# The order table of a fused retention and two-MLP kernel, replaced by another order of the same operations

## The chip, the cores and the metric

The kernel runs on one core of one Trainium2 chip. The metric is the device time of one execution, in microseconds (us): the median of several runs, shown with the lowest and the highest of them. One more execution was taken with the hardware profiler, and every row below is from that one.

## The reference

```python
# retention: B=2, H=8, S=768, D=64
gamma = 1.0 - 2.0 ** (-5.0 - np.arange(H))
for t in range(S):
    state = gamma * state + einsum('bhd,bhe->bhde', k[:, :, t], v[:, :, t])
    y[:, :, t] = D ** -0.5 * einsum('bhd,bhde->bhe', q[:, :, t], state)
x = y.transpose(0, 2, 1, 3).reshape(B * S, H * D)          # 1536 x 512

# MLP 1: w_in 512 x 2048, w_out 2048 x 512
h = x @ w_in
P = a[0] + a[1]*h + a[2]*h**2 + a[3]*h**3
Q = 1.0 + abs(b[0])*abs(h) + abs(b[1])*h**2
x = (P / (Q + 1e-6)) @ w_out

# MLP 2: the same sizes
h = x @ w_in2
out = (h / (1.0 + exp(-h))) @ w_out2
```

Everything is in fp32.

## The kernel before

**Retention.** The 768 positions of the two batches make 12 chunks of 128 (chunk c is position block c // 2 of batch c % 2). A chunk loads kT, qT, vn and kn (128x512 each) and goes through these operations. The *scores* are 16 matmuls of kT with qT (L435) into two PSUM banks. Two *masks* on VectorE (L317, tile `am`, in some chunks `u2` and `w`) multiply the scores with the causal decay in `msk`. The *decay of kn* is eight small scalings (L421), on ScalarE for the first chunks, which read their factors from `cst`. The *growth* is 16 matmuls of kn with vn (L468) and is what the state `bd` gains. The *outputs* are matmuls of vn with the masked scores (L480), and from the third chunk on with the state as well (L490). They land in bank `h1`, the growth in bank `h0`. ScalarE copies the outputs to `xh` (L309) and VectorE subtracts that copy to get `xl` (L317). These two are the high and the low half of x in the matmul format fp32r.

**The two MLPs.** Tokens form three groups of 512 (four chunks each), and d_ff is cut into 16 blocks of 128. That gives 96 *steps*, 48 for each layer. A step has a *first product* (L526): 12 matmuls of 128x512 into bank `h0` or `h1`, by turns of the step's number. They are three products, high by high, high by low and low by high, over four slices of d_model. Then comes a chain on ScalarE and VectorE (the rational function in layer 1, tanh and a multiplication in layer 2), which ends in `gh` and `gl`, and last the *accumulations* (L576): three matmuls into each of the four banks `acc0` to `acc3`, which are added up over the 16 blocks and then emptied. Bank h0 is free for the step after next only when the chain has read it for the last time.

**Weights.** A weight comes by DMA into one of three buffers `raw` (L343). ScalarE makes two pieces of it (`wt` and `raw`, L309), of which the second adds a constant, VectorE joins them (L324), ScalarE writes the high half (`ih`, `oh`, L386) and GpSimd or VectorE the low half (`il`, `ol`, L391). A weight that is needed again after its place is given away goes to DRAM as `spill` and comes back from there. All loads and stores are issued from SyncE (SP), in one queue. Two loads are tiny: `par` (the parameters of the rational function, broadcast to 128 partitions) and `cst`.

**What sets the order.** The program first lists all operations, each with the buffers that it reads and writes. Then `Flow.order()` decodes the table `ORDER`, a compressed list of 16-bit operation numbers, and the operations are emitted in that order:

```python
places = np.frombuffer(zlib.decompress(base64.b85decode("".join(ORDER))), np.uint16)
done = [self.ops[n] for n in places]
assert all(o.place < f.place for o in done for f in o.feeds)
...
with tc.manual_schedule():
    for o in flow.order():
        o.emit()
```

So an engine takes its instructions, and SP its transfers, strictly in the order of the table, and an instruction that has to wait holds up everything behind it on its engine. No other rule decides the order; the times and ranks that stand beside an operation in the code are not read when the table is used.

Of the kernel before, what the change touches and what calls it, by code (L numbers as in the profile page):

```python
# [27 lines left out]


ORDER = (  # L30
    'c-jru0|Foi3;@75d$w)cwr$(CZQHhO+qP}nZhtWo8bUxghyd|G03j>@gooG=2TsFoU?2zyksvZeflv@1B0?C53eh13oPo2D020ADhz5ILFT{lN',
    '5DWG}Lf8*!AQhy9xR4VvLM})RhanxLhYXMyl0ZJl1Zm+SB!`2L6pq3XNCqh&3uK4<Pymj>aVP;LArF*>+)x2Z!DYw{Wg#z|giBBm%D^G02&W(i',
    '6oz7O6|O*5C=cZz8&rZqP#lUtWdICNp#~g)n$R3-K`UqhwSf?^8ic@*_!f%7HMkB{fYG2TR0qLOSQqL+eYg!b!6AV6@D2<cKpk+r1+5`8HiCw5',
    '1H$78D2y$kJ#>d25FIbTNazWl;4^%Huy_aV!aaBZjiD(tgNPUbi{MAN4^1EvK7>c`7-C`!EQ)O)GIoG)*cLiMJLm*Y;3>qyV)zV-V{GgU@$m~p',
    '#jo%jzCl+giCv%@e1{*<2l_%UP#g}Wu`-6i5;zk^z%+=0<6s!X!7^AD6JSEDidFChl)~N+4f{h9OoU0XA5_C~SRKpbE69k6F&QSuOqdz7;7fP|',
    'uVDZTgxXjEr^9ks4dZbc)W8`q9DhOz%!Vm3J66P+m=%XW4$O&hu@2V7R5%m{K`zXVzn~J1f?7BW;^9B|4UKUEHo?@`6er>c9EpQrH2i_TP!IFq',
    'Sg4O<pcziW7B~tg<7k|Y^RY3F!3MY##zPwHiW6Z1q{p<_9J^t6%!|FSCHBCEI0ahaRP2eZaV$=PsW2IOV;`J}eK8+4!f7}TGhlv9hi$Me&V~Y5',
    '2;1RuY(fig1}?;v*dAA4KkSbKa1IQ_dC&m|;ZEF*yKoWC!o@fjR^b|4i>q-R?!mpd9{1sF+>aY@0d&MJI2ecFd?<*Wa3gNQ%Xk2n;z2xwO=&aE',
    '#l_H!4&xDA0t=xzJ;g<^0y^UmT!I~G6SSfpGzB-p9K4EG@CIJPo45+D<1>7LTW}f9!!>XVZ{te1gU|6OcB0nQhF)SXx{LSl6~4x{)R~UqR@{bb',
    'VI6$Oq4);h;t%XeKk+`E!sB=Xx8n|MM_s5Zy~FqT0Z(Il`h&mlH@2XU_yAkdCk#m!@GL&W-t-s$VIK-b>mdwnfW@?mPU0EdNI>ThDKssmix`%c',  # L40
    'P&gtAPZ200ZH7nq7@y#0WD@F2+n@s}^`qFdj3QBFib7jpD=eq9^aZ!WH@t*9=sd2b%@l{?QdHVRYbXJwqg@b>64F}QLhC3R#i#U?h!WF!+5s!*',
    'D;hb4pcoWTblOUpC<A4tB$SkPLNa<xuP7sBp{&%6c2RQ5M%gI`ZJ?FZol?+i+DZB84LzlTRDgC<MT$wWXb-)mcT|K5(KdQQIjJ%gre{=?icvLs',
    'PSt5I6{lRZk3LdjPD!aL4W**Il#g;#9x6d4sTB36&-95ZQBr<SNw^ACrP5S`zR*`n#x<!H)uuW$fCkbx8bU9qE)Al=G?a!>8TvpksUCf&a#WVe',
    '(?qI3^{Ejxqy{vcM$jahLL+GuO{L^KnWoWnO2uh-2F;|@oPtNw7}`!Lc|Xmf*))d^&_OyvhbS!{rHk}~a_~4BOXFz*0neqJoQp5fW%@-w=`bCm',
    'd31%Y(RKPw$LT5|-=LfHhfdH*O2?<@77;5m8%N{?w2)3ydXB_V_%;bUpP>w#k>|-mxkCX*=DQS?V{lB)#F_aXh2Ur$opW<Y4#lxJ3+Lhaw201A',
    'elE!8=mMRk0$h<F(F1x&p}7zj=J}GB|59wu%0;*+hv9r&j4N?vj>B<zkrd~6{EzNaIBw11IV@M<YFvV=b4f16ZMiDf;F?^T+i)4K#kIK|ci_I<',
    'j}veNPRQ-KKR4FXGFyJ|8R^8?c#hQJ1=5ih%K#q4gL$sh<)+%1vvWPZBIhKKi?T!#ae1!5<2gPL<RLtiCvX?;%H8;^Oyns%m51>p?#?~91ux|D',
    'vWUxZS#HYpxe;&X#oUZr@^D_l%XkDg;K@9V8}mqB&P#bZui%y3oEvg0Zo)Ho6mR7%e3X0gF`mh*couKt*}R>1@eV%0t9cHu;a)tNdvhNi%VT&P',
    '@8r3BosaWLKEu2DEU)ELe3~!F9^T9Acpu;7{d|MZ@p-<*clfH@=6k$U?(zX%z%O||&*SxcpI`At4lSGbFmK=^e1WgY8-Bpc<RZW3w|q%H@Fjl8',
    '@Ay4G;?zp|Pgwr)ZwVtGIjlV9PaIAn$P@m|mnEXal|y`$4{~^kB=ID^B#<whNd8D<0sYDeCA}n(zmiy@NK*O6$t0?z)60B~3(6IK%Fp>3zu@nj',  # L50
    'K{84v$s*Atxn!0?l1-vZb}1rRC5BWMk{pskib`QACOM_JG?fyPMpH_9ts*7mC#RBJQcX%pX%Q(Sf7m6qRF|sKOj<}S$t^9Vjf9X4`j68}Old25',
    '1U0RO6qVW%OKM1SsUvaZ7uS^3QdU|?8UZOMtlg!xnADX}GE&+}PwA|x^`wWimp;-<^2sRaEBU3jjFB$7T>41|87sfJzo1Nz0n%E#YDE!UA?akG',
    'WYLT|QS!<vsV@a&kgS&S(m+f*$|R{EqotEnl65j!8p}!<CrxCqbkjz%UdBrsZ76G`t?rZ|l2zAACY>T1WU92&>#|#>$u8L_`(%%Flbf<%y2=gN',
    'B%Nii+>w`ZKyJxFxhuED^`0D(CfZ$x$}2f6bG3`ymmc~?hD%R<Ae$x7UiwzH$Pt;ZGv%SYmJ!lSL+Cr1E+6EP%#x4tUWQ3?jj2Z^l(x{8+FOrF',
    'Xl<n-HJpag9TH1F$qWgv?RBfn)6X(hAImoBpkcM6o{}fhS5HVMjicKowjP%+5?7x|1f8zgG`oJ4h?+p-=`>BK-z2_1m7JPcPf8Arq%Wk8=F!Mn',
    'Qgdlu&8-VGpGMLA+E0H-X-%YqwUqYPayn3#>HsaHgS5Ps)$g)UpG#t0tj9H~F47q~MwjUlU9L%VrY6+_T0wuxTAiiIbhiGIA-Y1N=^Txr(RHjA',
    ')QXy1SL!-Vp+ohYuGdvMPE+a$t)yG^q!!ZET3HM08oi+Vbc3GPD!NgtY7yP6S9Oz~(p0)di|a5grWduSp4JjtO|R)4y`*Qfu3p#S`c-RbJw2<{',
    '^|IF223lKh=r$dtSG10f*X?>&N9sMDppW&N-qihiU;pTLJ)jNsht|-^+DLckB(15p^nt$7+xk$&{^~#dsgLxRhO*H*LU-yE{jCReqCQczr@C9s',
    '!1icpJEXfbjG-OXx9XPI$o6Vjd!~n#?VTRe_j*JF3uh56gr&0Qn$$8{NK0bjEt$o#NEX2&TN+DlsqKSCu^g7k(%K8nY*Fo%rm%GOQe#^dt7soJ',
    'y`{7`_F8k=XU%H4?2~4&xK_iyXf}&sxvi3Ax5}2^@>mtCW%Vtd)wB{;)e2Z%t8LA!n&q>CR><mDbZcPMt)ca|m{!*kT1hKx(X55lvr?AGnp=D;',  # L60
    'ZH+8}wX^|N%o^K3Yh`V%i4C_h*4oBfQyXO6tev&7_BO%>+eqtRLu`~yx1m<VI@&}lZli62mA7HG(Z<>sn`9NNyN$D=HrdMB4C`S#ZN5#lDb~}b',
    '*(U2{n{B3Tu`ag2W?5I;Wm|29?Y4z>(ze?++haRyua&dew%_(yKU--B?SL(^Io8Qm*<9;vi>;QQwt05ZPFY=FZD(wa9k#P}$f|oEJ7<^dh%LAC',
    'cG>#c1-oTO?YJGYu71LL+iiPockGHa@T>O4-q>6FYqh<G*YTR(+k5y1TVl&>tu3`{cGuR~JzH;I?Ye!lcXrd>+kN|I?%)sXp@sKu-qX8#FAo)j',
    '4Q|*A`)(iXhrP6?_R0ePY$5!a{j}#6!ynlndu-^R?8*Nq`)I!{f`{~o{>vJAC})r4jXa^p^vGV%gCLgI_kJGQ6S;X}7f<DxT|Jz~_AuVZ<9Jx_',
    '>#048M+nk*5|8HnJ*nsM0iMN^23b9-7xm~K-_v?rPv`MGuP5+)p3Jj(InVCJytpU#6rR#Ecz#ds1w50N_l#b_b9)KT<t4q1=kUf}#G80dZ|ViT',
    'q7U>+-qzdsC@<xOy{s4VYTnGtcyq7pgS@H__7*<dOM7c??^V2mxAGz0(MS7G@9blIj<@u=zQo7+IPc<1Jw(vSmwD)5n1>AJd6;0hrwHczcuyUy',
    '^$9-FxA{6>?;|{AFw&C+se(zKJXr2ieT7f<1wO^6`F3CE(|w1}@cq8QXZl8;<tO}rAM}g9$`|=!U+Fu2jfV?%`6dq^ob=V6E;!{|{g7|=h{0js',
    ';*o+&zQ-^7X}{&^gEO8Xc<i_Rj_>t1e$4mzc|Y#E{it8@Bc3L>>gPOdaM#cJ6Tjy-{Hee73;xc(`ZIs-*ZrIS^Y8x9ulY^C@9+JUfA9zY7dUc&',
    'L7d=`fA$~#+JE{>j}m<GsKFo482t4Y{>dr$=p6j^Xu&U!8$=H@h!<oEB#0km4srzv0uOQrF@ijS1qp*JLF^!F5GzO$#0+u<d4t43z93PMEhrJ>',
    '2ucR|gHl2Epg>SGC>Rt9iUq}k!a<SXKT#GXzW',  # L70
)


# [663 lines left out]
```

## Time and profile before

| | before |
|---|---|
| median of 3 runs | 600.87 us (598.21, 601.35, 600.87) |
| the profiled execution | 599.9 us |
| its span in the trace | 598.1 us |
| mean granted clock of TensorE | 0.991 of full speed |
| busy: PE, DVE, ACT, POOL | 579.3, 426.7, 396.9, 134.8 us |

PE is TensorE (its matmuls), PEld its weight loads, DVE is VectorE, ACT ScalarE, POOL GpSimd, and SP the queue of transfers. The span runs from the first to the last instruction of the trace; the profiled execution's time is 1.8 us longer, for what lies around it. A busy time counts from the start to the end of instructions, and matmuls are pipelined, so a matmul shows a longer duration than the distance to the next one. A granted clock of 1.0 is 2.4 GHz, one of 0.5 is 1.2 GHz.

### The profile page before, as it was taken

Reading aid. Unit: us, or ns where it says so; the run is one execution under the profiler, and the core shown is the slowest. Engines: PE = TensorE matmul, PEld = TensorE weight load, DVE = VectorE, ACT = ScalarE, POOL = GpSimd, SP = SyncE. Lnnn points to the kernel's source line nnn. Section 1 sums busy time; section 2 is a strip of 40 time slices with the busy share of each in tenths; the row PEclk is TensorE's granted clock in tenths of the full one; section 3 lists DMA queues with packets and bytes.
Section 4 is the critical chain, followed back from the end, with each engine's and each line's share of the span. In section 5 each row is a group of like instructions: output and inputs, shape, how many; then the busy total and the mean of one; then the engine's idle time right before and its main releaser. Section 6 shows DMA issues by size and latency. Waiting matters only on the chain.

```text
span 598.1 us, 8106 instructions
## 1 busy us (share of the span) xinstructions
PE 579.3 (97%) x2950; PEld 475.6 (80%) x2950; DVE 426.7 (71%) x646; ACT 396.9 (66%) x690; POOL 134.8 (23%) x104
## 2 busy tenths in 40 slices
...
GB/s 291 326 330 302 337 140 169 169 134 78 105 72 81 96 1 105 18 19 107 53 106 158 176 135 187 195 222 176 71 89 36 1 1 0 106 18 1 0 2 71
DMA packets 33368, 70.02 MB, mean 117 GB/s; under 512 B 3632, under 2 KB 3632, under 8 KB 33328
## 3 DMA queue, kind: packets, MB, share of 16 engines
...
## 4 chain that ended last, share of the span: by engine, by line
PE 57%; DVE 17%; DMA 13%; ACT 9%; issue 2%; SPq 2%; ACTq 0%; DVEq 0%
PE acc L576 28%; PE h L526 27%; DMA raw<-in_moe_w_in_dram 6%; DVE wt L324 4%; DVE s L324 3%; DMA raw<-in_moe_w_out_dram 3%; DMA spill<-wt 2%; SPq L343 2%; DVE s L317 2%; DVE gl L317 1%; ACT wt L309 1%; ACT raw L309 1%; DVE u L324 1%; DVE t L324 1%; DVE r L324 1%
## 5 line engine op out<-in xcount | busy, mean ns | idle before, releaser
L526 PE MATMUL h<-xh,ih 128*128 128x512 f32 x384 | 150.7, 392 | 2.2 <-DVE s L324 1.9
L526 PE MATMUL h<-xl,ih 128*128 128x512 f32 x384 | 149.5, 389 | 0.0
L526 PE MATMUL h<-xh,il 128*128 128x512 f32 x384 | 149.5, 389 | 0.0
L317 DVE TENSOR_TENSOR gl<-w,gh 128x512 fp32r<-128x512 f32 x48 | 34.2, 712 | 82.5 <-ACT gh L309 82.4
L526 PEld LDWEIGHTS h<-xh,ih 128*128 128x128 f32 x384 | 72.1, 188 | 20.7 <-DVE s L324 3.6
L526 PEld LDWEIGHTS h<-xh,il 128*128 128x128 f32 x384 | 72.1, 188 | 15.1
L526 PEld LDWEIGHTS h<-xl,ih 128*128 128x128 f32 x384 | 72.1, 188 | 14.5
L309 ACT ACTIVATE gh<-w 128x512 fp32r<-128x512 f32 x48 | 30.2, 629 | 80.3 <-PE acc L576 77.0
L576 PE MATMUL acc<-oh,gh 128*128 128x512 f32 x192 | 74.8, 390 | 1.4 <-DVE xl L317 1.4
L576 PE MATMUL acc<-gh,oh 128*128 128x512 f32 x192 | 75.9, 395 | 0.0
L576 PE MATMUL acc<-gh,ol 128*128 128x512 f32 x192 | 74.8, 390 | 0.0
L576 PE MATMUL acc<-gl,oh 128*128 128x512 f32 x192 | 74.8, 390 | 0.0
L576 PE MATMUL acc<-ol,gh 128*128 128x512 f32 x192 | 74.7, 389 | 0.0
L576 PE MATMUL acc<-oh,gl 128*128 128x512 f32 x192 | 74.7, 389 | 0.0
L391 POOL TENSOR_TENSOR ol<-wt,oh 128x512 fp32r<-128x512 f32 x28 | 40.0, 1431 | 119.3 <-ACT oh L386 114.9
L324 DVE SCALAR_TENSOR_TENSOR w<-w,h 128x512 f32<-128x512 f32 x48 | 32.8, 685 | 37.6 <-ACT w L309 37.0
L324 DVE SCALAR_TENSOR_TENSOR wt<-wt,raw 128x512 int32<-128x512 int32 x64 | 50.4, 796 | 10.4 <-ACT wt L309 5.7
L309 ACT ACTIVATE raw<-raw,par 128x512 int32<-128x512 uint32 x64 | 48.4, 761 | 10.0 <-DMA raw<-in_moe_w_in_dram 5.2
L309 ACT ACTIVATE w<-h 128x512 f32<-128x512 f32 x48 | 28.3, 593 | 35.9 <-PE h L526 25.0
L317 POOL TENSOR_TENSOR gl<-s,gh 128x512 fp32r<-128x512 f32 x26 | 35.2, 1356 | 69.9 <-ACT gh L309 47.0
L309 ACT ACTIVATE wt<-raw 128x512 f32<-128x512 f32 x64 | 42.2, 666 | 12.3 <-DMA raw<-in_moe_w_in_dram 5.3
L324 DVE SCALAR_TENSOR_TENSOR s<-s,par,h 128x512 f32<-128x512 f32 x65 | 48.2, 743 | 0.9
...
## 6 DMA issues: line engine op xcount, KB each, us to landing
...
```

The costliest lines, as they stand in the source:

```text
L309: lambda: nc.scalar.activation(out=out_, in_=in_, func=func, **kw),
L317: op(eng, dur, rank, lambda: e.tensor_tensor(out=out_, in0=in0, in1=in1, op=alu), reads, writes, port)
L324: lambda: nc.vector.scalar_tensor_tensor(out=out_, in0=in0, scalar=scalar, in1=in1, op0=op0, op1=op1),
L343: op("swdge" if swdge else "sync", us, rank, lambda: e.dma_start(out=out_, in_=in_), reads, writes)
L391: e.tensor_tensor(out=sl.t[nm + "l"][:, us], in0=wt.t, in1=sl.t[nm + "h"][:, us].bitcast(F32), op=ALU.subtract)
L526: nc.tensor.matmul(h.t, sl.t[w][:, ws], x[g].t[:, c, :], start=(n == 0), stop=(n == 3 * KD - 1))
L576: nc.tensor.matmul(a.t, a1, a2, start=(first and n == 0), stop=(last and n == 2))
```

## The change

Only the strings of the table `ORDER` differ. The operations, their buffers and what each computes are the same, and so is the number of instructions on every engine. What differs is the place of an operation in its engine's queue: of PE's 515 operations 430 stand at another number than before, of ACT's 659 565, of DVE's 646 530, of GpSimd's 100 58, and of SP's 203 transfers 166.

```diff
@@ -28,46 +28,46 @@
 ORDER = (
-    'c-jru0|Foi3;@75d$w)cwr$(CZQHhO+qP}nZhtWo8bUxghyd|G03j>@gooG=2TsFoU?2zyksvZeflv@1B0?C53eh13oPo2D020ADhz5ILFT{lN',
...
+    'c-jru0}dbw5CFh-&)T+a+qP}nwr$(CZQHhO`|cB!R0s$Kp&=Zch6sQV2f{*Z0Eh?SVK=0Lj6lE;5+XrlhyrKeEJTDb5FZjiA~**LAsR%5J+K#I',
...
 )
```

The largest shift is at the start. On SP, the queue of transfers, these are the first eleven before (qT, kT, kn and vn are the chunks' inputs, `raw_2` of `moe_w_out` and `raw_0` of `moe_w_in` the first weights, the number in a name is that of the buffer):

```order
L343 DMA qT_0_168<-in_qt_dram 128x512
L343 DMA kn_0_162<-in_k_dram 128x512
L343 DMA kn_1_163<-in_k_dram 128x512
L343 DMA par_65<-in_moe_a_dram 128x4
L343 DMA cst_63<-in_consts_dram 128x48
L343 DMA kT_0_171<-in_kt_dram 128x512
L343 DMA msk_64<-in_consts_dram 128x1024
L343 DMA vn_0_165<-in_v_dram 128x512
L343 DMA kT_1_172<-in_kt_dram 128x512
L343 DMA qT_1_169<-in_qt_dram 128x512
L343 DMA raw_2_126<-in_moe_w_out_dram 128x1024
```

and these after the change:

```order
L343 DMA qT_0_168<-in_qt_dram 128x512
L343 DMA raw_2_126<-in_moe_w_out_dram 128x1024
L343 DMA kn_0_162<-in_k_dram 128x512
L343 DMA cst_63<-in_consts_dram 128x48
L343 DMA qT_1_169<-in_qt_dram 128x512
L343 DMA kT_0_171<-in_kt_dram 128x512
L343 DMA kT_1_172<-in_kt_dram 128x512
L343 DMA msk_64<-in_consts_dram 128x1024
L343 DMA kn_1_163<-in_k_dram 128x512
L343 DMA vn_0_165<-in_v_dram 128x512
L343 DMA raw_0_124<-in_moe_w_in_dram 128x2x512
```

The first half of a weight pair now stands second, both kT follow each other at the places 6 and 7, kn_1 has moved from the third to the ninth place, vn_0 from the eighth to the tenth, and `par` from the fourth to the 28th.

On ACT, these are the first instructions of the program before (L421 decays kn, L309 on `wt` and `raw` are the pieces of a weight, `xh0` is the copy of the outputs of chunk 1, `bd0` the state):

```order
L421 ACT_TABLE_LOAD
L421 ACTIVATE kn_1_163<-kn_1_163,cst_63 128x64 x8
L421 ACTIVATE kn_0_162<-kn_0_162,cst_63 128x64 x8
L309 ACT_TABLE_LOAD
L309 ACTIVATE u2_0_132<-u2_0_132,par_65 128x1
L309 ACTIVATE bd0_160<-h0_155 64x4x64 x2
L309 ACTIVATE wt_2_129<-raw_2_126 128x512
L309 ACTIVATE raw_2_126<-raw_2_126,par_65 128x512
L309 ACTIVATE wt_0_127<-raw_0_124 128x512
L309 ACTIVATE raw_0_124<-raw_0_124,par_65 128x512
L309 ACTIVATE xh0_66<-h1_156 128x4x128
```

and after the change:

```order
L309 ACT_TABLE_LOAD
L309 ACTIVATE wt_2_129<-raw_2_126 128x512
L309 ACTIVATE raw_2_126<-raw_2_126,par_65 128x512
L421 ACTIVATE kn_0_162<-kn_0_162,cst_63 128x64 x8
L309 ACT_TABLE_LOAD
L309 ACTIVATE u2_0_132<-u2_0_132,par_65 128x1
L421 ACTIVATE kn_1_163<-kn_1_163,cst_63 128x64 x8
L309 ACTIVATE wt_0_127<-raw_0_124 128x512
L309 ACTIVATE raw_0_124<-raw_0_124,par_65 128x512
L309 ACTIVATE xh0_66<-h1_156 128x4x128
L309 ACTIVATE bd0_160<-h0_155 64x4x64 x2
```

ACT's first instructions now read `raw_2` and no longer `kn_1` and `cst`; the two decays of kn lie between the pieces of the first two weights, and the copy to `bd0` comes behind xh0.

On DVE, this is the place in step 36's chain (layer 1, third group) where bank h0 (`h0_155`) is read for the last time, before (`raw` here holds the sums of the first group, `il` is a low half of a weight):

```order
L317 TENSOR_TENSOR raw_2_126<-acc1_152,raw_2_126 128x512
L317 TENSOR_TENSOR gl_1_147<-s1_1_137,gh_1_144 128x512
L391 TENSOR_TENSOR il3_85<-wt_1_128,ih3_84 128x512
L391 TENSOR_TENSOR il2_81<-wt_4_131,ih2_80 128x512
L317 TENSOR_TENSOR s1_0_136<-s1_0_136,h0_155 128x512
L324 SCALAR_TENSOR_TENSOR t_0_141<-u2_0_132,r_1_140 128x512
L324 SCALAR_TENSOR_TENSOR s1_0_136<-s1_0_136,par_65,h0_155 128x512
```

and after the change:

```order
L317 TENSOR_TENSOR raw_2_126<-acc1_152,raw_2_126 128x512
L391 TENSOR_TENSOR il2_81<-wt_0_127,ih2_80 128x512
L391 TENSOR_TENSOR il3_85<-wt_1_128,ih3_84 128x512
L324 SCALAR_TENSOR_TENSOR r_0_139<-t_1_142,r_0_139 128x512
L324 SCALAR_TENSOR_TENSOR u2_0_132<-w_0_134,par_65,h0_155 128x512
L317 TENSOR_TENSOR s1_0_136<-s1_0_136,h0_155 128x512
L324 SCALAR_TENSOR_TENSOR s1_1_137<-s1_1_137,par_65,r_1_140 128x512
L324 SCALAR_TENSOR_TENSOR s1_0_136<-s1_0_136,par_65,h0_155 128x512
L324 SCALAR_TENSOR_TENSOR s1_2_138<-s1_2_138,par_65,r_0_139 128x512
L317 TENSOR_TENSOR gl_1_147<-s1_1_137,gh_1_144 128x512
```

The last row of the first piece is the last read of h0 for step 36, after which PE may write the bank again. It stands at row 369 of DVE before and at row 362 after; `gl_1`, and the low half from `wt_4`, which stood ahead of it, now stand behind it.

On PE, the shifts that matter are these. Chunk 5's scores stood ahead of step 0's first product and now stand behind it. In chunks 0 and 1 the outputs now stand ahead of the growth. Between the first products of steps 2 and 3 there are three accumulations where there was one. At step 36 to 40, other matmuls have moved ahead of the first products of steps 38 and 40 (9 more of them, 2.0 us, and 18 more, 4.1 us). In the second layer most first products stand some accumulations later than before. The end of the program is practically the same.

## Rows read from the trace of the kernel before

**Rows 1.** The page: busy time of each engine, share of the span, instructions.
```profile
PE 579.3 (97%) x2950; PEld 475.6 (80%) x2950; DVE 426.7 (71%) x646; ACT 396.9 (66%) x690; POOL 134.8 (23%) x104
```

**Rows 2.** Busy time in three long stretches; the last columns are clock, DMA, GB/s.
```profile
core 0: us, PE busy (x) PEld busy (x) DVE busy (x) ACT busy (x) POOL busy (x), PEclk, DMA share, GB/s
0.00:60.00 60.00, 47.82 (x467) 40.97 (x468) 41.67 (x72) 43.83 (x93) 25.59 (x25) 0.91 0.90 313
60.00:280.00 220.00, 218.78 (x1111) 177.50 (x1111) 211.68 (x328) 193.96 (x329) 72.88 (x55) 1.00 0.33 110
280.00:598.00 318.00, 312.69 (x1375) 257.16 (x1373) 173.35 (x250) 159.07 (x269) 36.33 (x24) 1.00 0.27 85
```

**Rows 3.** Whom PE waited for: us in total, times, longest.
```profile
PE h L526 <- DVE s L324: 1.9, 3, 0.9
...
```

**Rows 4.** The same columns as rows 2, in the first 15 us.
```profile
0.00:4.00 4.00, 2.52 (x12) 2.52 (x13) 0.54 (x2) 0.00 (x0) 1.19 (x6) 1.00 0.57 162
4.00:6.00 2.00, 2.00 (x12) 1.96 (x11) 0.00 (x0) 0.00 (x0) 0.00 (x0) 1.00 0.67 113
6.00:7.00 1.00, 0.15 (x2) 0.00 (x0) 0.00 (x0) 0.26 (x1) 0.00 (x0) 1.00 0.84 314
7.00:15.00 8.00, 5.82 (x54) 5.32 (x56) 1.75 (x4) 7.92 (x23) 0.00 (x0) 0.63 1.04 398
```

**Rows 5.** The same columns, in the two stretches with the low clock.
```profile
9.10:15.80 6.70, 5.46 (x46) 5.12 (x48) 2.19 (x5) 6.63 (x19) 0.00 (x0) 0.50 1.01 376
46.60:49.90 3.30, 3.18 (x34) 2.88 (x35) 2.30 (x5) 2.32 (x5) 1.77 (x2) 0.50 1.03 387
```

**Rows 6.** PE's timeline, first 60 us: start, duration, instruction [idle before, releaser].
```profile
7.79 1.16 PE L435 MATMUL a<-qT,kT 64*128 64x128 f32 x16 [1.65 <-DMA kT<-in_kt_dram]
...
10.34 2.14 PE L468 MATMUL h<-vn,kn 128*64 128x64 f32 x16 [1.38 <-ACT kn L421]
...
19.42 0.32 PE L480 MATMUL h<-u,vn 128*64 128x128 f32 x1 [1.53 <-DVE u L317]
...
31.86 0.47 PE L526 MATMUL h<-xh,ih 128*128 128x512 f32 x1
...
39.61 1.09 PE L480 MATMUL a<-am,vn 128*64 128x128 f32 x16
...
43.96 1.16 PE L435 MATMUL a<-qT,kT 64*128 64x128 f32 x16 [1.56 <-DVE bd L317]
46.72 1.12 PE L468 MATMUL a<-vn,kn 128*64 128x64 f32 x16 [1.59 <-DVE am L317]
47.59 1.95 PE L480 MATMUL a<-am,vn 128*64 128x128 f32 x16
```

**Rows 7.** PE's timeline, later: matmuls in a row, and three waits.
```profile
261.71 0.39 PE L576 MATMUL acc<-gl,oh 128*128 128x512 f32 x1
...
262.39 0.39 PE L576 MATMUL acc<-gl,oh 128*128 128x512 f32 x1
263.42 0.50 PE L526 MATMUL h<-xh,ih 128*128 128x512 f32 x1 [0.65 <-DVE s L324]
...
270.87 0.50 PE L526 MATMUL h<-xh,ih 128*128 128x512 f32 x1 [0.35 <-DVE s L324]
...
343.64 0.51 PE L576 MATMUL acc<-oh,gh 128*128 128x512 f32 x1 [1.35 <-DVE xl L317]
```

**Rows 8.** ACT's timeline in the first 18 us, same columns.
```profile
6.74 1.28 ACT L421 ACT_TABLE_LOAD   x1 [6.74 <-DMA cst<-in_consts_dram]
8.03 3.92 ACT L421 ACTIVATE kn<-kn,cst 128x64 f32<-128x64 f32 x16
...
14.24 0.67 ACT L309 ACTIVATE wt<-raw 128x512 f32<-128x512 f32 x1
14.82 0.75 ACT L309 ACTIVATE raw<-raw,par 128x512 int32<-128x512 uint32 x1
...
16.84 0.60 ACT L309 ACTIVATE xh<-h 128x512 fp32r<-128x512 f32 x1
```

**Rows 9.** The masks in the view of tile msk: duration ns min/median/max, starts.
```profile
L317 DVE TENSOR_TENSOR am<-a,msk x18: 673/682/692, 9.4 to 125.5; 128x512 f32<-128x512 f32 x18
```

More of the change, by code (lines that the diff above doesn't have):

```diff
@@ L30 @@
 ORDER = (
-    'c-jru0|Foi3;@75d$w)cwr$(CZQHhO+qP}nZhtWo8bUxghyd|G03j>@gooG=2TsFoU?2zyksvZeflv@1B0?C53eh13oPo2D020ADhz5ILFT{lN',
[L32 to L70, printed above, removed]
+    'c-jru0}dbw5CFh-&)T+a+qP}nwr$(CZQHhO`|cB!R0s$Kp&=Zch6sQV2f{*Z0Eh?SVK=0Lj6lE;5+XrlhyrKeEJTDb5FZjiA~**LAsR%5J+K#I',
@@ new lines @@
+    'LUf1)`(Qt$gt(9ka>8Lq4QU`9WPtRL1Y*EJNDhf1DI|j<a1`=E3dj!y;5;0IOmGMaLKa91+2J_kfD%v=@<48=0Hq*6fdg<EN&}$6MaT;$p)6#E',
+    'a*!3uLpHbs72y<=fx=J>LShIk1Vx}SRD&yU6^cS}2!)}sI$Q&T>+lvTK^3S4C!hw@gjUcTYD0Lu4Tyve0lbHIz*rRo>%s^41a}}T-h{gl0b4@@',
+    'r~|hk9M*?=&<GkrbZiM1paryt!gvD|dq8)%2lpW&HiZZ95I(~rh>4FO27Uy?FVGm8K@*6CZQuz+#tz`v7CJ&Z=mcM(C>Ft|@C@Q(EG&kdAvSh}',
+    'ZtxtUVi)KGVX!pzg334ydcrp-j^806Cc%<e7877x`~g3q3YNjD_yYPvZ}<hT;SIcmjMxv7Vj}Dd<**u-$Lg3EGht?|h_7G({Dyz<2L{4l7y%<8',
+    '3f9Kq7zc;LI4FTNa6Ha{=}-YHVJVD;@o*Gm!z`E`lVNg9fmtyJ=ENb85>sJntb-%5F6P3aFbD=iZp?%AurW5pCO86X;zXQ)qoF>Ig)z_!Ti_^c',
@@ new lines @@
+    'iIZ?NPR5xq4W{E#n2*b#F*U&PkOsSAcbo`QU;?DabeI-1U|wvF-LMso#nw0#C&6Tx3caug_Qp1t4{PB#oQC;vHWb1FSP<J{J6w)EaR&CmzSs{J',
+    ';!IqC?Xf=&z*)EgS7JjPh;v{r%*Hji2v^}+oCh6n5H`YDuoHLTZd{G~a1ZXsb+{fk;6~hpi*YYDp{8^I58@&0gq?8#bj0~E1iRo|yo`tO2sWeU',
+    'v=E-+Qd|s6;3{s$qj&`u!415IH*p1Qf{ic-r{HqvNUNb0^`J4h0k+_CT!!;-4IIN~cpW>@EqsNmU?sf97ucC@;~l(<ZKxLw!=X4Bx8V-lil=Zb',
+    '9LJZ~noi>z>`8C2E#1TKxE=3fJL*mE@I8LO_H+V&;yU<&E$Ab5p{~@2e&HYdi|gSxKERgr2}4q73Ps^43|+v7corYwXWR@YaS5Km#k7hx(mw=3',
+    'A_`AS=p0_eu(XsSP()(d3d`s*KEb}Un%0m|2igYxNGUdb!AKODqR?_mOIu(Q#ia!F4Y$L2+(DNxDs84+5QkP!I!aG#X$!5Rc$AQ~QhZuZi6}7{',
```

29 lines of the change are left out of this document (added).

## The prediction

> **What bounds the kernel now.** I read the page first, then the span in three long stretches, then who PE waited for, and last the timelines of the start. The page says that PE is busy for 97% of the span, DVE for 71% [rows 1]: the matmuls are the bound, and an order can only give back time in which PE stands still or runs slowly. The three stretches show where that is [rows 2]. In the first 60 us PE is busy for 47.82, so 12.2 us are idle. From 60 to 280 us it misses 1.2 us of 220, and from 280 on 5.3, the end of the program included. The list of PE's waits agrees: thirteen kinds, 15.0 us together, of which the longest in total stands here [rows 3]. The DMA column tells why the start is slow: 313 GB/s over the first 60 us against 110 afterwards [rows 2]. Finer windows show that the transfers themselves lose time: 398 GB/s once they stream, but 113 between 4 and 6 us [rows 4], where the 16-byte pieces of `par` and the 24 KB of `cst` are in the queue and little else. To the idle time comes slow time: the granted clock is 0.50 (1.2 GHz) from 9.1 to 15.8 us and again from 46.6 to 49.9 us [rows 5]. In the first of these the 16 growth matmuls of chunk 0 take 2.14 us, in the second those of chunk 6 1.12 and its first 16 output matmuls 1.95 [rows 6]. PE was busy for 3.18 us of the second stretch, so the low clock cost half of that there, 1.6 us.
>
> DVE matters too: busy for 211.68 of the 220 us from 60 to 280 [rows 2]. Where PE stands still behind the start, it waits for DVE: at 263.42 and 270.87 for the last read of an h bank, 1.0 us together, and at 343.64 for an xl that frees an accumulator, 1.35 us [rows 7]. The same group gives the price of matmul work at full clock: four of 128x512 in a row start within 0.68 us, so an accumulation (three) takes 0.68 and a first product (twelve) 2.7.
>
> **The change, part by part.** No instruction is added or removed, so it costs and saves only through places in the queues.
>
> *The start.* Five transfers stand ahead of the first kT in either order, but what they carry differs. Before, 1075 KB had to pass up to the first kT's own end (three of 262 KB, `par`, `cst` and kT itself). The windows give 648 KB by 4.0 us and 874 by 6.0, so the 1075th passed at 6.64 [rows 4]; the scores began at 7.79 [rows 6], a lag of 1.15 us, which I add to each landing below. After the change, 524 KB of `raw` stand second and `par` stands far back. I take it that the dip between 4 and 6 us goes with `par`, since the queue ahead of it is then full, and let the stream run at 398 GB/s from 4.0 us on. Kept wholly, the dip costs about 1.1 us (226 KB in 2.0 us instead of 0.9 us' worth).
>
> The first kT ends at 1597 KB: 4.0 + (1597 - 648)/398 + 1.15 = 7.5, so the first scores start 0.25 us earlier. The second kT is next, 262 KB on, where it stood ninth: the scores of chunk 1 run at 8.7, where before they stood behind the growth of chunk 0. The first vn ends at 2907 KB, 10.8 us, and the outputs of chunk 0 start there, at 10.9, ahead of the growth that they stood behind.
>
> ACT decides from there. Before, it sat until `cst` had landed, loaded its table, decayed both kn (3.92 us for 16), loaded again, and only then reached the weights; it copied the first xh at 16.84 [rows 8]. Now its first wait is for `raw`: 786 KB, 5.5 us. Table 1.28, the two weight operations 0.67 and 0.75, eight decays 2.0, table and one element 1.6, eight more decays 2.0, two weight operations 1.3: 15.1 us, and xh ends at 15.7 where it ended at 17.44. DVE's xl takes 0.7, as a mask does [rows 9], and the outputs of chunk 1 start at 16.4 instead of 19.42 [rows 6]: 3.0 us ahead. The same walk goes on over chunk 2 (scores 14.2, masks to 18.9, xl to 19.5, outputs 19.6: 2.7 ahead), ACT's decay of kn 2 (to 22.9), its xh and DVE's xl to 24.2, outputs of chunk 3 at 24.3 (2.6 ahead), growth of chunk 3, outputs of chunk 4 to 29.0. There the first product of step 1 begins, which began at 31.86 [rows 6]: 2.9 us.
>
> Then something is given back. Before, the scores of chunk 5 stood ahead of step 0's product, which covered the two mask multiplications; now they stand behind it, and the two masks at 0.68 each [rows 9] lie open ahead of chunk 5's outputs: 1.4 us of idle PE. I get 37.7 for those against 39.61 [rows 6], 1.9 ahead. Chunk 6 keeps its two waits. At step 2's product the new order has 2 us if the clock falls there as it did, and 3.5 to 4 if it does not. Between steps 2 and 3 PE runs three accumulations where it ran one: 1.4 us that no longer wait for step 1's chain. **I take 3.0 us for the start**; the bounds are nothing (all lost again by step 3) and 5.2 (full clock, plus the accumulations).
>
> *Steps 36 to 40.* DVE's last read of bank h0 for step 36 stands seven rows earlier, and PE calls the product of step 38, which waits for it, after 2.0 us more of other matmuls; step 40's comes 4.1 us of work later. The waits there are 0.65 and 0.35 us [rows 7], so they should go: **1.0 us**, between nothing and 1.0.
>
> *The turn of the layers.* The xl that PE waited 1.35 us for stands at the same row of DVE, and PE comes to the accumulator one accumulation (0.68) sooner: a wait of 2.0, with 0.68 of other work now behind it. **Nothing gained**; bounds -0.7 and +1.35.
>
> *The second layer.* PE does its first products later against the accumulations, by 2 to 10 us of matmul work, and so comes later to weights that may not have landed. Hardly anything waits there now, so this buys nothing in a run in which nothing is late. A step's chain (tanh, multiply, gh, gl) is four operations on 128x512, 0.6 to 0.8 us each where the rows show such ones [rows 8, 9], about 3 us; the shortest run of matmuls between a step's first product and its own accumulations is 5.4 us (7.5 before): covered. If one such cover failed, PE would wait at most that chain, 3 us.
>
> *Unknown small waits* among 500 moved rows: the old order left those three, 2.35 us, behind the start [rows 7]. I take back **0.4**, bounds 0 and 2.35.
>
> The sum is 3.0 + 1.0 + 0 - 0.4 = 3.6 us. The profiled execution took 599.9 us (span 598.1), so 596.3. The median of the runs, 600.87, lies 1.0 higher, and the profiled one within their spread; I name 596.7.
>
> **The rivals.** *The lead is eaten by DVE.* PE can keep 3 us only if DVE has them too, and DVE has 8.3 idle us between 60 and 280 [rows 2]. For it: it is DVE that PE waits for there. Against it: DVE's end of step 1's chain comes about 3 us sooner in the same walk, and nothing is put on DVE. Then only the 1.0 remains: 599 or a little more. To the same time leads that the new start does not do what it says, for instance because the streams still dip without `par`.
>
> *The clock, and a slower kernel.* Chunk 5's new wait and chunk 6's two lie within 9 us. Before, the clock was low from 46.6 us, after two waits of 1.56 and 1.59 us in chunk 6 [rows 5, 6]. If it falls at chunk 5 and stays at 1.2 GHz until step 2's product is done, 9.2 us of matmuls (outputs 2.1, growth 0.6, scores 1.1, growth and outputs 2.7, product 2.7) take twice as long: 599.9 - 1.9 - 1.0 + 0.4 + 9.2 - 1.6 (what the old low stretch cost) = 605. It turns the sign once about 5 us of matmuls on the path run at half clock beyond those of before. The Trainium skill ("TensorE: Matmul & The Clock Gate", the section "Loop structure matters more than you think") holds that matmuls back to back keep the clock up and that long waits for transfers let it fall. By it, waits as short as these would leave the clock alone, there would be no such rival, and the new start would keep all of the 3.9 us at step 2: 595.4. The trace shows the clock fall behind two short waits, so I keep the rival.
>
> *Everything works.* 5.2 + 1.0 + 1.35 = 7.55: 592.4.
>
> **How the numbers follow.** My forecast gets 0.56 (594.5 to 598.5 by its own bounds), the lost lead 0.26 (599 to 601), the clock 0.08 (602 to 605), the full gain 0.10. A measurement of this kernel tells about 0.5%, 3.0 us, from no change: faster is below 597.9. Of my own case some 0.85 lies there, with the full gain 0.58. Between 597.9 and 603.9 lie the rest of it and the lost lead, 0.34; slower gets 0.08. The range 593.0 to 600.8 leaves out a tenth on either side.
>
> **What would show it.** Right: transfers at about 390 GB/s without a dip before 15 us; outputs of chunk 1 near 16.4, step 1's product near 29, chunk 5's outputs with a wait of about 1.4 us ahead, PE idle for 8 to 10 us in the first 60; no PE wait for DVE between 255 and 275; one of 1 to 2 us at the turn. Wrong: PE ahead at 60 us but with new waits for DVE behind it (DVE is the bound), a clock of 0.50 between 38 and 50 us over a longer stretch than before, or waits in the second layer for gl.

## The result, and the profile after the change

| | before | after |
|---|---|---|
| median, first comparison (6 and 6 runs) | 598.52 us (596.11 to 601.35) | 593.05 us (591.04 to 593.81) |
| ratio to before | | 0.9895 (95%: 0.9861 to 0.9929) |
| a second comparison, run changed_again (23 and 6 runs) | 599.26 us (596.48 to 602.01) | 592.33 us (589.87 to 593.66) |
| ratio to before | | 0.9879 (0.9855 to 0.9903) |
| profiled execution, its span | 599.9, 598.1 us | 591.33, 589.5 us |

The kernel became 1.1% faster: 5.5 us between the first two medians, to 593.05, where I had forecast 596.7 (3.2 us below the profiled execution's 599.9). The runs of the new order also lie closer together.

The page and the three long stretches of the changed kernel, as in [rows 1, 2]:

```profile
PE 574.0 (97%) x2950; PEld 474.0 (80%) x2950; DVE 417.5 (71%) x646; ACT 394.2 (67%) x690; POOL 132.9 (23%) x104
```

```profile
0.00:60.00 60.00, 48.78 (x499) 41.60 (x499) 45.37 (x77) 47.12 (x100) 24.98 (x26) 0.97 0.89 317
60.00:280.00 220.00, 220.00 (x1109) 180.25 (x1108) 211.03 (x328) 192.72 (x325) 72.08 (x56) 1.00 0.33 109
280.00:589.50 309.50, 305.23 (x1346) 252.13 (x1344) 161.12 (x243) 154.32 (x267) 35.87 (x24) 1.00 0.27 87
```

From 60 to 280 us PE doesn't stand still at all. In the first 60 it is idle for 11.2 us, only 1.0 less than before [rows 2]. But it did more in that time (499 matmuls, 467 before), and the clock was higher: 0.97 against 0.91. PE's list of waits has nothing left from behind 60 us (us in total, times, longest):

```profile
PE acc L435 <- DMA kT<-in_kt_dram: 1.8, 1, 1.8
PE a L435 <- DVE bd L317: 1.6, 1, 1.6
PE h L480 <- DVE am L317: 1.6, 1, 1.6
PE a L468 <- DVE am L317: 1.5, 1, 1.5
PE h L644 <- DVE par L648: 1.5, 1, 1.5
PE a L480 <- DVE am L317: 1.4, 1, 1.4
PE a L435 <- DMA kT<-in_kt_dram: 0.8, 1, 0.8
PE a L435 <- DMA qT<-in_qt_dram: 0.8, 1, 0.8
PE h L480 <- DMA vn<-in_v_dram: 0.3, 1, 0.3
```

PE's timeline has the times that the prediction named, as in [rows 6]:

```profile
7.31 1.16 PE L435 MATMUL a<-qT,kT 64*128 64x128 f32 x16 [0.83 <-DMA kT<-in_kt_dram]
...
15.48 0.32 PE L480 MATMUL h<-u,vn 128*64 128x128 f32 x1
...
27.58 0.49 PE L526 MATMUL h<-xh,ih 128*128 128x512 f32 x1
...
36.66 1.09 PE L480 MATMUL a<-am,vn 128*64 128x128 f32 x16 [1.39 <-DVE am L317]
...
41.01 1.16 PE L435 MATMUL a<-qT,kT 64*128 64x128 f32 x16 [1.56 <-DVE bd L317]
43.66 0.98 PE L468 MATMUL a<-vn,kn 128*64 128x64 f32 x16 [1.49 <-DVE am L317]
```

The outputs of chunk 1 run at 15.48 (16.4 forecast), step 1's product at 27.58 (29), and those of chunk 5 wait 1.39 us for their masks (1.4).

**Lost time by stretch.** To add up idle and slow time, I take the distance from the start of each piece of PE's program to the start of the next, less what the piece takes at full clock (product 2.72, accumulation 0.68, scores 1.09, growth 0.60, outputs 0.98, with state 1.94). The sum over a stretch is what was lost there. With 570.0 us of work (7.3 of them stand for the time up to the first scores) it gives the end of the last matmul in every run. Us, from each kernel's profiled execution, which need not lie at the median: those of changed_again and turn2_new are the fastest of their runs, that of before lies 0.6 us above the median of the second comparison.

| kernel | 0-60 | 60-140 | 140-250 | 250-300 | 300-360 | 360-end | sum | ratio of the runs |
|---|---|---|---|---|---|---|---|---|
| before | 16.1 | 2.9 | 0.3 | 2.3 | 1.7 | 1.0 | 24.3 | 1 |
| changed | 12.1 | 2.3 | 0.3 | 0.0 | 0.0 | 0.6 | 15.4 | 0.9895 |
| changed_again | 10.7 | 2.3 | 0.6 | 0.0 | 0.1 | 0.2 | 13.9 | 0.9879 |
| ret_new | 12.8 | 3.2 | 0.3 | 2.2 | 1.7 | 0.2 | 20.3 | 0.9942 |
| ret_old | 18.3 | 3.8 | 0.3 | 0.0 | 0.1 | 0.2 | 22.7 | 0.9974 |
| turn2_new | 14.0 | 3.7 | 0.8 | 0.6 | 0.4 | 0.2 | 19.8 | 0.9971 |
| s51_late | 14.4 | 2.6 | 0.4 | 0.0 | 2.4 | 0.2 | 19.9 | 0.9916 |

### The profile page after: what moved, and what is told of

It reads as the page before. It is cut to its first block, busy times and chain, and to the rows that moved or that the text cites. A ratio compares the mean times of both kernels' runs of the same rounds, so it can differ in the third digit from the quotient of the medians.

```text
span 589.5 us, 8100 instructions
## 1 busy us (share of the span) xinstructions
PE 574.0 (97%) x2950; PEld 474.0 (80%) x2950; DVE 417.5 (71%) x646; ACT 394.2 (67%) x690; POOL 132.9 (23%) x104
## 4 chain that ended last, share of the span: by engine, by line
PE 91%; DMA 4%; DVE 2%; ACT 1%; issue 1%; SPq 0%; ACTq 0%
PE acc L576 43%; PE h L526 43%; DMA kT<-in_kt_dram 2%; PE a L490 2%; PE a L435 2%; PE a L480 1%; DVE wt L324 1%; DMA raw<-in_moe_w_out_dram 1%; DMA qT<-in_qt_dram 1%; PE a L468 1%; SPq L343 0%; ACT raw L309 0%; DVE am L317 0%; DVE w L324 0%; PE h L468 0%
## 5 line engine op out<-in xcount | busy, mean ns | idle before, releaser
L526 PEld LDWEIGHTS h<-xh,ih 128*128 128x128 f32 x384 | 72.1, 188 | 16.1 <-DVE s L324 0.6
L309 ACT ACTIVATE w<-h 128x512 f32<-128x512 f32 x48 | 28.1, 593 | 78.7 <-PE h L526 74.2
L391 POOL TENSOR_TENSOR ol<-wt,oh 128x512 fp32r<-128x512 f32 x28 | 38.6, 1389 | 105.6 <-ACT oh L386 94.4
L309 ACT ACTIVATE gh<-w 128x512 fp32r<-128x512 f32 x48 | 29.8, 629 | 46.7 <-PE acc L576 31.6
L324 DVE SCALAR_TENSOR_TENSOR wt<-wt,raw 128x512 int32<-128x512 int32 x64 | 45.0, 707 | 12.0 <-ACT raw L309 7.2
L391 POOL TENSOR_TENSOR il<-wt,ih 128x512 fp32r<-128x512 f32 x28 | 39.5, 1419 | 51.3 <-ACT ih L386 34.2
L309 ACT ACTIVATE raw<-raw,par 128x512 int32<-128x512 uint32 x64 | 48.1, 758 | 1.5 <-DMA raw<-in_moe_w_in_dram 0.8
L317 POOL TENSOR_TENSOR gl<-s,gh 128x512 fp32r<-128x512 f32 x26 | 35.2, 1353 | 59.4 <-ACT gh L309 37.7
```

Source lines behind the costliest of these rows:

```text
L309: lambda: nc.scalar.activation(out=out_, in_=in_, func=func, **kw),
L317: op(eng, dur, rank, lambda: e.tensor_tensor(out=out_, in0=in0, in1=in1, op=alu), reads, writes, port)
L324: lambda: nc.vector.scalar_tensor_tensor(out=out_, in0=in0, scalar=scalar, in1=in1, op0=op0, op1=op1),
L391: e.tensor_tensor(out=sl.t[nm + "l"][:, us], in0=wt.t, in1=sl.t[nm + "h"][:, us].bitcast(F32), op=ALU.subtract)
L526: nc.tensor.matmul(h.t, sl.t[w][:, ws], x[g].t[:, c, :], start=(n == 0), stop=(n == 3 * KD - 1))
```

## The experiments

Each table of these kernels is put together from the two tables, `old` and `new`. `then` takes what is not yet there in the order of the next one. Ratios are to before, on the same chip.

**Pieces cut at a step of PE.** Four kernels take one stretch from the new order:

```diff
 start_new = new up to step 4's product, then old
 start_old = old up to step 4's product, then new
 mid_new   = old up to step 32, then new up to step 44, then old
 turn_new  = old up to step 46, then new up to step 54, then old
```

> The changed kernel's order up to the first product of step 4 (about 60 us), the old order behind it. Theory A, each stretch keeps what its own order gives: PE's waits for VertorE's chain at step 38, step 40 and the turn of the layers stay as they were (0.65, 0.35 and 1.35 us, to within 0.5), the lead at step 30 is 4 to 5 us, and the profiled execution takes 595.5 to 596.5 (3.5 to 4.5 below 599.9). Rival B, VectorE is the bound from 60 to 280 us and eats the lead: the waits for it behind 60 us grow by 3 us or more together, and the time is 598.5 to 600.

> The complement: the old order up to the first product of step 4, the changed kernel's behind it. Theory A: no wait of PE for VectorE behind 100 us, although PE has no lead from the start; 4 to 5 us below before (594.5 to 596 against 599.9). Rival B, the waits of steps 38 and 40 and of the turn went because the new start brought everything forward, not because of the order there: they come back, 2 us or more together, and the time is 597.5 to 599.

> The old order with the changed kernel's only from step 32's first product to step 44's (230 to 290 us). Theory A: the waits at steps 38 and 40 go and the small losses around them (1.6 us from 260 to 280, 0.3 from 240 to 260, 0.4 from 280 to 300), the time falls by 1.5 to 2.3 us: 597.6 to 598.4 against 599.9. Rival B: at least one of the two waits stays, gain below 0.8 us. The wait of 1.35 us at the turn stays in both.

> The old order with the changed kernel's only from step 46's first product to step 54's (308 to 360 us), where step 51's first product now stands between the last accumulations of layer 1 and the first of layer 2. Theory A: that product, 2.7 us, covers the subtraction that frees the accumulator, the wait of 1.35 us goes with the 0.35 around it, 1.7 us less: 598.2 against 599.9. Rival B, as I predicted: the wait stays at 1 to 2 us or moves to another accumulator, gain below 0.7.

Measured: start_new 0.9991 (0.9961 to 1.0021), start_old 0.9987 (0.9956 to 1.0017), mid_new 1.0037 (1.0009 to 1.0064), turn_new 0.9977 (0.9954 to 1.0000). Only turn_new came out near theory A. In mid_new the waits of steps 38 and 40 went, but new ones of 0.83 and 0.86 us came at the products of steps 33 and 45, so the time rose. In start_new this stands at the seam, in PE's timeline:

```profile
74.91 1.16 PE L490 MATMUL a<-qT,bd 128*128 128x128 f32 x8 [1.93 <-POOL qT L317]
76.00 0.78 PE L468 MATMUL a<-vn,kn 128*64 128x64 f32 x16
76.71 0.79 PE L576 MATMUL acc<-gh,oh 128*128 128x512 f32 x1
77.30 0.63 PE L576 MATMUL acc<-gh,ol 128*128 128x512 f32 x1
77.73 0.63 PE L576 MATMUL acc<-gl,oh 128*128 128x512 f32 x1
```

A wait for GpSimd, and behind it accumulation matmuls that start 0.43 us apart and not 0.23: half clock. A table cut where the two orders have done different things makes waits of its own, so these ratios don't price the pieces. What they do show is where the late waits belong. In start_new, with a new start, PE waits 0.62, 0.33 and 1.34 us at step 38, step 40 and the turn as before; in start_old, without it, none of the three is there. Rival B (the new start brought everything forward) falls.

**Pieces cut where both orders have done the same.** At places 570 and 1520 of the table (131 and 355 us) only one operation each way tells what the two orders have done by then, at 1080 (249 us) three.

```diff
 ret_new   = new[:570], then old
 ret_old   = old[:570], then new
 turn2_new = old[:1080], then new[:1520], then old
 changed_again = new
```

> The changed kernel once more, on the same chip as the next three and as more runs of before: 592 to 594 at the median against 599 to 600, with runs that lie closer together than those of before, and hardly a loss of TensorE behind 60 us. Theory A: its start is less sensitive to when transfers land, so the loss in the first 60 us varies by less than 2 us between this profile and the first one (12.1 us). Rival C: the first profile was lucky there (clock 1.00 from 9 to 16 us), and the loss is 14 us or more.

> The changed order for the first 570 places of the table (to 131 us, the whole retention and steps 0 to 11), the old one behind it; the two orders have there done the same operations but one each, so the seam moves nearly nothing. Theory A: what is lost in the first 140 us falls from 19.0 us to 14.5, the waits of steps 38 and 40 and of the turn stay (0.65, 0.35, 1.35 us): 595 to 596 in the profiled execution, a ratio of 0.993 in the runs. Rival B: VectorE eats the lead, the waits behind 131 us grow by 2 us or more and the ratio is 0.998 or above.

> The complement, the old order for the first 570 places and the changed one behind. Theory A: the loss of the first 140 us is that of before, 17 to 20 us, and behind it less than 1 us is lost: 595.5 to 596 against 599.9, ratio 0.993; the two halves together give the whole. Rival D: the halves don't add up, most of the 1% (0.990 or below) needs the one of them alone and the other has a ratio above 0.998.

> The old order, with the changed one only from place 1080 to 1520 (249 to 355 us: steps 36 to 53, the turn of the layers among them), where the seams move 6 and 2 operations. Theory A: the waits of steps 38 and 40 and of the turn all go and none takes their place: 3.5 to 4 us less, 596 to 596.4 against 599.9, ratio 0.994. Rival E: new waits at other first products take half of it or more, as they did where the piece was cut with larger seams: gain below 2 us, ratio 0.997 or above.

Measured: changed_again 0.9879, ret_new 0.9942 (0.9920 to 0.9964), ret_old 0.9974 (0.9953 to 0.9996), turn2_new 0.9971 (0.9954 to 0.9988). For ret_new theory A holds in the main. Its start has the gain (16.0 us lost in the first 140, where theory A said 14.5 and before has 19.0), and PE's late waits are those of before: 0.62 us at step 38, 0.35 at step 40, 1.35 at the turn. The third wait of the first line, 0.42 at 132.87, is new and stands right behind the seam:

```profile
PE h L526 <- DVE s L324: 1.4, 3, 0.6
PE acc L576 <- DVE xl L317: 1.4, 1, 1.4
```

VectorE did not eat the lead (rival B). ret_old missed the 0.993 of its theory A. Its profile has no late wait left and lost 4.7 us less than before's behind 140 us, but 3.1 more ahead of it (22.1 against 19.0) with the same order there. The medians, too, are only 1.5 us apart, so this isn't the chance of one profile alone; what makes up for the late gain is not shown. The two halves make 0.9942 x 0.9974 = 0.992, against 0.988 and 0.990 for the whole, within the intervals. turn2_new is rival E by its ratio (0.997 or above, a gain below 2 us). In its profile the waits of steps 38 and 40 and of the turn are gone, and 1.5 us of small losses came.

Executions differ at the start even with the same order. These are the 20 us windows of changed_again (columns as in rows 2):

```profile
0.00:20.00 20.00, 13.81 (x169) 12.74 (x170) 9.12 (x17) 14.19 (x35) 5.25 (x9) 1.00 0.95 344
20.00:40.00 20.00, 17.39 (x200) 14.42 (x198) 17.26 (x31) 16.85 (x39) 10.28 (x9) 1.00 0.96 338
40.00:60.00 20.00, 17.44 (x150) 14.01 (x151) 19.81 (x33) 17.48 (x31) 10.88 (x10) 1.00 0.84 293
```

The clock stayed at 1.00, and the span was 588.1 us. (The three other profiles that kept it at 1.00 in the first 20 us had 0.66, 0.50 and 0.50 from 43 to 48 us; changed_again's 1.00 there is the exception.) Theory A's claim of a start that varies by less than 2 us holds for these two (12.1 and 10.7), but s51_late, with the same start, lost 14.4.

**Transfers or engines.** Up to place 570, sp_new has SP's queue from the new order and the other engines from the old one, and sp_old the reverse.

```diff
 up to 131 us:  SP   PE, ACT, DVE, GpSimd
 sp_new         new  old
 sp_old         old  new
```

> Up to place 570 of the table (131 us) SP issues the transfers in the changed order, and all other engines go by the old one; the rest is as before. With its complement, the next run, it splits the gain of the new start (ratio 0.994). Theory G: the two belong together; ScalarE still begins with the decay of kn_1, which now lands later (the ninth transfer, about 10 us), so the start loses: the outputs of chunk 1 at 21 us or later (19.4 before) and a ratio of 1.002 to 1.008. Rival H: the transfers alone bring the gain: ratio 0.996 or below.

> The complement: up to place 570 SP in the old order, all other engines in the changed one. Theory G: ScalarE's first work now reads raw, the eleventh transfer of the old queue (about 10 to 11 us), so the decays of kn come 4 us late: outputs of chunk 1 at 21 us or later, ratio 1.003 to 1.010. Rival I: what the engines do first is all that counts, and the order of the transfers little: ratio 0.997 or below.

Measured: sp_new 1.0215 (1.0188 to 1.0242), sp_old 1.0316 (1.0285 to 1.0347). Both are slower, as theory G had it, and by more than it said. ACT's timelines show the start of it, in the changed kernel, in sp_new and in sp_old:

```profile
4.90 0.66 ACT L309 ACTIVATE wt<-raw 128x512 f32<-128x512 f32 x1 [2.89 <-DMA raw<-in_moe_w_out_dram]
...
6.12 2.00 ACT L421 ACTIVATE kn<-kn,cst 128x64 f32<-128x64 f32 x8
...
13.45 0.58 ACT L309 ACTIVATE xh<-h 128x512 fp32r<-128x512 f32 x1
```

```profile
10.27 3.92 ACT L421 ACTIVATE kn<-kn,cst 128x64 f32<-128x64 f32 x16 [2.69 <-DMA kn<-in_k_dram]
```

```profile
11.82 0.67 ACT L309 ACTIVATE wt<-raw 128x512 f32<-128x512 f32 x1 [9.81 <-DMA raw<-in_moe_w_out_dram]
...
16.57 2.00 ACT L421 ACTIVATE kn<-kn,cst 128x64 f32<-128x64 f32 x8
```

Whichever half is missing, the first thing that ACT does waits for a transfer that stands behind others. The loss goes on beyond the start: sp_old loses 10.9 us between 60 and 140, with a wait of 4.87 for chunk 8's masks. DVE's masks stood there behind a piece of a weight, for which ACT had waited 6.55 us, until 83.84, for `raw`: the engines ask for transfers in an order in which SP doesn't issue them.

**The dip.** Only the load of `par` is moved, in the old order.

```diff
 L343 DMA kn_1_163<-in_k_dram 128x512
-L343 DMA par_65<-in_moe_a_dram 128x4
 L343 DMA cst_63<-in_consts_dram 128x48
```

> The old order, with one thing moved: the load of par (2 KB, 16 bytes for each partition) goes from the fourth place of SP's queue to the 28th, where the changed order has it. Theory A, as in my prediction: the dip to 113 GB/s between 4 and 6 us goes with it, the first kT lands about 1 us earlier (scores at 6.7 instead of 7.8), ScalarE's first decay of kn too, and the loss of the first 140 us falls by about 1 us: ratio 0.998. Rival F: the streams dip anyway or a later transfer sets the start, the scores begin at 7.5 or later in the profile and the ratio is 1.000.

Measured: 0.9993 (0.9970 to 1.0015). The dip went, 357 GB/s between 4 and 6 us where before had 113 [rows 4]:

```profile
4.00:6.00 2.00, 2.00 (x11) 2.00 (x11) 0.00 (x0) 0.97 (x1) 0.00 (x0) 1.00 1.06 357
6.00:7.00 1.00, 0.55 (x3) 0.25 (x2) 0.00 (x0) 0.99 (x4) 0.00 (x0) 1.00 0.96 221
```

But the scores began at 7.24, between theory A's 6.7 and rival F's 7.5, and no gain can be measured. The mechanism is there; its price is below what the runs can tell. ret_old shows that the dip also varies: with `par` in fourth place it had 239 GB/s in that window.

**The clock at the start.** Before stood still for 1.65 us ahead of the first scores [rows 6]. warm_more shortens that to 0.99 us with more matmuls on zeros (the number counts pairs of them):

```diff
-'wm': 11
+'wm': 14
```

> The old order and one number changed: 28 instead of 22 matmuls on zeros ahead of the first scores, so that TensorE is busy until about 7.5 us and doesn't stand still for 1 to 2.5 us there. Theory J: that stand is why the granted clock falls to 0.50 around 9 to 16 us in the old order; without it the clock of the first 20 us is 0.95 or more, where before's 0.84 was, and the start loses up to 2.5 us less: ratio 0.996 to 0.998. Rival K: the clock falls for what comes later (the waits for the decay of kn and for the masks), it stays low somewhere in the first 20 us, ratio 1.000.

Measured: 0.9994 (0.9973 to 1.0014). The clock fell all the same (0.75 from 9.1 to 15.8 us, growth of chunk 0 in 2.00 us): rival K. A stand of 0.99 us was left, so this run alone does not exclude theory J. But start_new, with the new order at the start, stood still for 1.74 us ahead of its first scores, and its clock was 1.00 over the first 20 us. The other way round, one step of the changed order is put back on PE:

```diff
 scores of chunk 0
-scores of chunk 1
 outputs of chunk 0
 growth of chunk 0
+scores of chunk 1
```

> The changed order, and on TensorE alone one step moved: the scores of chunk 1 stand behind chunk 0's outputs and growth, as in the old order, and not behind chunk 0's scores. TensorE then stands still for about 2.5 us at 8.4 us. Theory M: the clock falls there as in the old starts; granted clock of the first 20 us 0.93 or less, outputs of chunk 1 at 17 us or later (15.5 in the changed kernel), ratio to before 0.991 to 0.995. Rival N: the clock stays at 1.00, outputs of chunk 1 at 16 to 16.8, ratio 0.988 to 0.990.

Measured: 0.9940 (0.9915 to 0.9965), about 3 us slower than the changed kernel. The outputs of chunk 1 ran at 18.7, and the clock was 0.83 in the first 20 us. Theory M's numbers, but its cause is not shown, because the clock was already low before the step that was moved, when the first kT came late:

```profile
8.25 1.58 PE L435 MATMUL a<-qT,kT 64*128 64x128 f32 x16 [2.20 <-DMA kT<-in_kt_dram]
```

The profile of s51_late, whose start is the changed one untouched, has the same thing: kT late, a wait of 2.19 us, and a low clock (scores in 1.47 and 1.98 us).

**The turn of the layers.** In the changed order, step 51's product alone moves on PE.

```diff
 last accumulation of step 47 (layer 1)
-first product of step 51
 two accumulations of step 48 (layer 2)
+first product of step 51
```

> The changed order, and on TensorE alone one step moved: step 51's first product stands behind the first two accumulations of layer 2 and not ahead of them. Theory A: that product was the cover; TensorE now waits at the first or second of these accumulations for VectorE's subtraction (done at 333.2 and 333.8 in the changed kernel, TensorE there at 331.8): 1.2 to 1.5 us, and the ratio to before is about 0.991 where the changed kernel has 0.988. Rival L: VectorE's order alone did it, no wait above 0.4 us there.

Measured: 0.9916 (0.9884 to 0.9948), with PE's timeline at the turn, in the changed kernel and in s51_late:

```profile
331.58 0.39 PE L576 MATMUL acc<-gl,oh 128*128 128x512 f32 x1
331.81 0.39 PE L526 MATMUL h<-xh,ih 128*128 128x512 f32 x1
...
334.53 0.39 PE L576 MATMUL acc<-oh,gh 128*128 128x512 f32 x1
```

```profile
334.14 0.39 PE L576 MATMUL acc<-gl,oh 128*128 128x512 f32 x1
335.86 0.50 PE L576 MATMUL acc<-oh,gh 128*128 128x512 f32 x1 [1.33 <-DVE xl L317]
336.20 0.39 PE L576 MATMUL acc<-ol,gh 128*128 128x512 f32 x1
```

The wait is back at 1.33 us, where the old order had 1.35 [rows 7], and the stretch from 300 to 360 loses 2.4 us (1.7 before, nothing in the changed kernel); 0.6 of it goes with a second, smaller wait of this kind at 346.08. In the new order the product was the cover (theory A); the trace shows it, while the intervals of the two ratios overlap. The fastest runs agree: 591.8 against 589.9.

In the old order the size of this wait hung on VectorE. Between its two subtractions stands a joining of a weight's pieces, which took 1.80 us in before and about as long in six other profiles that have the old order at the turn. In the eighth, par_late, it took 0.85, PE lost 0.22 us at this place, and the stretch from 300 to 360 lost 0.4 and not 1.7. DVE's timelines in before and in par_late:

```profile
340.58 0.69 DVE L317 TENSOR_TENSOR xl<-acc,xh 128x512 fp32r<-128x512 f32 x1 [0.99 <-ACT xh L309]
341.19 1.80 DVE L324 SCALAR_TENSOR_TENSOR wt<-wt,raw 128x512 int32<-128x512 int32 x1
342.91 0.68 DVE L317 TENSOR_TENSOR xl<-acc,xh 128x512 fp32r<-128x512 f32 x1
```

```profile
339.64 0.69 DVE L317 TENSOR_TENSOR xl<-acc,xh 128x512 fp32r<-128x512 f32 x1 [2.76 <-ACT xh L309]
340.25 0.85 DVE L324 SCALAR_TENSOR_TENSOR wt<-wt,raw 128x512 int32<-128x512 int32 x1
341.02 0.68 DVE L317 TENSOR_TENSOR xl<-acc,xh 128x512 fp32r<-128x512 f32 x1
```

So the old order need not lose 1.7 us here in every execution. Why that operation is long is not shown: in before a low half on GpSimd begins 0.04 us ahead of it, at 341.15, but no run tests whether that is the reason.

## Why the prediction was wrong, point by point

- **What bounds the kernel** was right: PE at 97%, and the whole gain is idle or slow time of PE given back. It came to 8.9 us between the two profiles (24.3 to 15.4) and 5.5 to 6.9 between the medians, where I had 3.6.
- **The step that failed is the turn of the layers**, put at "Nothing gained" because PE would come one accumulation sooner. I had counted accumulations only and missed that the new order puts step 51's product, 2.7 us, between the last accumulation of layer 1 and the first of layer 2. The wait of 1.35 us went, 1.7 with the slow restart behind it (the second matmul starts 0.34 us after the first and not 0.23), and s51_late brought 1.33 back by moving that product. I also took the 1.35 for a cost of the order; in before, most of it came from one long operation of DVE that par_late's profile does not have.
- **Steps 36 to 40** were right in kind and too small in size, 1.0 against 2.3. In DVE's queue the last read of h0 stands five rows earlier, at 364, and not seven: row 362 is the read before it. In the changed kernel DVE begins it at 255.46, PE comes at 259.70, and the stretch from 250 to 300 loses nothing. The old order lost more there than its two waits: 0.3 us within the accumulations at 259, 0.4 at 299, and 0.1 at each restart.
- **Unknown small waits**, 0.4 taken back, was wrong in sign: no wait of 0.15 us or more stands behind 60 us in the changed kernel, and 60 to 140 us got 0.6 better.
- **The start**, 3.0 us, measured 4.0 between the profiles, but by another split. The times of the walk came 0.9 to 1.4 us early (forecast 16.4, 29 and 37.7, measured 15.48, 27.58 and 36.66), but its path did not hold. ACT's first table load, which I had put behind `raw` with 1.28 us, ran at 0.73 while ACT waited for `raw`, and xh of chunk 1 began at 13.45 (its row stands under "Transfers or engines"), not at 15.1. PE no longer waited for it: chunk 1's outputs stand behind chunk 2's scores, and these waited for a transfer:

```profile
0.73 1.28 ACT L309 ACT_TABLE_LOAD   x1 [0.73 <-PEq L714]
```

```profile
14.39 1.16 PE L435 MATMUL acc<-qT,kT 64*128 64x128 f32 x16 [1.82 <-DMA kT<-in_kt_dram]
```

  PE was idle for 11.2 us where I had 8 to 10. Three of the four us are slow time: the stretch from 9.1 to 15.8 us at 0.50 [rows 5] was at 1.00, as the changed kernel's windows show, and only the second low stretch is still there:

```profile
9.10:15.80 6.70, 3.33 (x61) 2.94 (x60) 4.79 (x8) 5.05 (x15) 0.17 (x1) 1.00 1.05 396
43.00:48.00 5.00, 4.34 (x42) 3.97 (x43) 3.82 (x8) 2.32 (x5) 2.38 (x2) 0.66 0.83 314
```

  I had counted a full clock only at step 2, as a bound. That this is part of the gain is read from the profiles; no experiment here controls the clock. But it is more than one pair of profiles: the first 20 us have 0.83 or 0.91 in all eight that begin in the old order (par_late and warm_more among them), and 1.00 in four of the five that begin in the new one as it is (s51_late has 0.91).
- **The dip** of `par` went as forecast, but by itself it is worth nothing that can be measured. The 1.1 us that I named for it don't follow from my rows: 226 KB at 398 GB/s are 0.57 us, so 1.4 of the 2.0 us would be lost. The sum doesn't use that figure.
- **The rivals.** The lead was not eaten: ret_new keeps it with the old DVE order behind it. The clock did not fall longer: 43 to 48 us at 0.66 in the first profile, 1.00 in the second. "Everything works", 592.4, was the case that came (593.05 and 592.33), and I had given it 0.10. That its time fits is in part luck: in the profiles the start gave 4.0 where that case has 5.2, steps 36 to 40 gave 2.3 for 1.0, and the turn 1.7 for 1.35. I took back bounds that my own counts of the order, read to the end, would have given.

**What stays open**: why the clock stays up in the new start when the first kT comes in time (PE stood still there for 1.55 and 1.82 us within the same 7 us), whether the halves add up exactly (the intervals allow it), and why ret_old gains only 1.5 us without a late wait.
